# Weaving softmax steps into a 7-product matmul: later attention blocks, debits for mask sums, spread loads, and diagonal copies on GpSimd

## The chip, the core and the metric

The kernel runs on one core of one Trainium2 chip. A core has a matmul engine (TensorE, PE in the profile), two elementwise engines that do most of the rest (VectorE, DVE, and ScalarE, ACT), a third (GpSimd, POOL) and a sequencer that here only issues DMAs (SyncE, SP). Each engine works through its own instructions in order; across engines they wait for each other by semaphores. The metric is device time of one execution in microseconds.

## The reference

Windowed attention over 8 batches, 8 heads, 576 positions of 64 features, then a two-layer perceptron with an ELU on the 4608 resulting tokens of 512 features. All in float32.

```python
scores = scale * q @ k.T                                # per batch and head, 576 x 576
mask_plain = (rel >= 0) & (rel < 32)                    # heads 0 to 3, rel = row - column
mask_dil = (rel >= 0) & (rel < 32 * 4) & (rel % 4 == 0) # heads 4 to 7
scores = where(mask, scores, -1e9)
scores = scores - max(scores)
attn = exp(scores)
attn = attn / (sum(attn) + 1e-9)
x = (attn @ v), heads side by side: (4608, 512)
h = x @ w_in                                            # (512, 2048)
g = where(h > 0, h, exp(min(h, 0)) - 1)
out = g @ w_out                                         # (2048, 512)
```

## The kernel before, in words

Every float32 matmul is made of three matmuls of a shorter format (each operand is split into a rounded part, by a "cast", and a "rest"). The tokens come in two ways: three plain chunks of 512 tokens first, then four groups of 768 tokens (`superchunk(c)`, c = 0 to 3), of which this change concerns the first three.

In a group the first layer is done with seven products instead of eight, in Strassen's manner. There are 8 quarters q, each with 7 products s. `ORDER` names the weight combination of each (`A11 S2 S3 A12 S1 A22 S4`, DMA'd ahead into a ring of `r` tiles by `load_combined`, from the tensor `combined`), `MOVING` the token operand (`B11 T2 T3 B21 T1 T4 B22`). A product is six matmuls of 128x384; the products accumulate in PSUM in `x_ps` (tile `h`) or `y_ps` (tile `a_ps` or `h`). `TODO[s]` lists what follows product s on the other engines: `u1`, `u2`, `u3` are ScalarE copies out of PSUM, `C11`, `C22`, `C12` VectorE adds out of PSUM, `C21` a ScalarE copy; then exp, relu, cast on ScalarE and elu, rest on VectorE; `keep` sends half of the result to `aside` in memory. TensorE can start the next product into a PSUM tile when these reads are done. Products of the second layer (three matmuls of 128x512 each) wait in a list and are put between the others by `pop`. Behind the 8 quarters comes a loop of 16 steps f, in which the kept halves come back from `aside` (`bring`), are cast and rested (tiles `gh`, `gl`), and the operands of the next group are made (`OPERANDS[f]`).

The attention of batches 4 to 7 is woven into this. It is cut in 8 blocks, each of two head pairs; block i has a scores piece `S<i>` and an outputs piece `O<i>`. `PIECES[c]` says behind which product (index 7q+s) of group c a piece stands, `LATER` behind which f. An S piece puts the score matmuls (`o_ps<-kt,qt`, `a_ps<-kt,qt`) on TensorE; half way a GpSimd memset clears the first column of one `kt`, and the remaining score matmuls read it. Six VectorE adds of masks (L381) follow. The rest of the softmax is put in a list, `side`, by `later_probabilities`: per pair a maximum, a subtract, an exp on ScalarE, a sum, +1e-9, a reciprocal, a multiply, two 32x32-block transposes, and six copies of the diagonal blocks into a tile `pt`. The first pair uses tile `sm` and `pt_79`, the second tile `a` and `pt_78`. An O piece multiplies `pt` by `vt` (`a_ps<-pt,vt`).

What sets the order: `work(vec, act)`, once behind each product (`SPARE[s]` holds the two numbers, in us), adds `vec` to a running credit and runs steps from `side` as long as credit remains, and ScalarE steps within `act`. `work_all`, ahead of each piece, runs everything left of the blocks before it (of its own block too, for an O piece): a flush. `Ordered` (L430) ties each instruction it issues into this written order on its engine; that is why so many instructions of the profile have L430 as their line, and the matmuls L110.

q, k and v of later blocks are fetched by `load_qk` and `load_v`, at the end of an S or O piece: four or two DMAs at once on SyncE's queue, which carries the ring's and `aside`'s transfers, too.

Of the kernel before, what the change touches and what calls it, by code (L numbers as in the profile page):

```python
# [44 lines left out]
CS = 3  # L45
# [6 lines left out]
POPS = (2, 2, 0, 0, 0, 2, 0)  # L52
FIRST_POPS = (2, 2, 0, 0, 0, 0, 0)
TODO = [t.split() for t in ("u1 exp0< relu0< w0", "u2 elu0< cast1< cast0< rest1< rest0< w1", "u3 keep1< w2", "C11 w3", "C22 keep0< expR1 w4", "C21 expL1 relu1 w5 push1", "C12 elu1 w6 push0")]
SPARE = ((1.4, 0.45), (0.3, 0.9), (1.2, 1.3), (1.6, 1.7), (0.9, 0.5), (0.9, 0.0), (0.0, 0.45))
SOON = "cast:B11 make:T1 rest:B11 make:T2 cast:T2 rest:T2 make:T3 cast:T3 rest:T3".split()
FIRST = [t.split() for t in ("cast:B21 rest:B21", "make:T4 cast:T1 rest:T1", "cast:T4 rest:T4", "cast:B22 rest:B22", "", "", "")]
OPERANDS = [t.split() for t in ("", "", "", "cast:B11", "make:T1 rest:B11", "make:T2 cast:T2", "rest:T2 make:T3", "cast:T3 rest:T3", "cast:B21 rest:B21", "make:T4 cast:T1",
                                "rest:T1", "cast:T4 rest:T4", "cast:B22", "rest:B22", "", "")]
WHEN = {1: (0, 6, 7, 13), 2: (0, 6, 7, 12)}  # L60
EARLY = 14
LAST = 14
OPER = 12
PLAIN = ("a5", "a-1'")
BLOCKS = [(b, hp) for b in range(CS + 1, B) for hp in (0, 2)]
PIECES = {0: {14: "S1", 20: "O0", 28: "S2", 34: "O1", 42: "S3", 48: "O2"}, 1: {7: "S4", 28: "S5", 34: "O4", 48: "O5"}, 2: {7: "S6", 28: "S7", 34: "O6", 48: "O7"}}
LATER = {0: {3: "O3"}}
COMBINE = {(1, 11): 0, (1, 13): 1, (1, 15): 2, (2, 1): 3, (2, 4): 4, (2, 6): 5, (2, 9): 6, (2, 11): 7}

TINY = float(np.array([0x38000000], np.uint32).view(np.float32)[0])  # L70
# [3 lines left out]
def body(ctx: ExitStack, tc: tile.TileContext, q, k, v, masks, w_in, w_out, out):  # L74
# [184 lines left out]

    qk_of, v_of = {}, {}  # L260

    def load_qk(i):
        if i < B * NPAIR:
            qt, kt = qk_of[i] = ap.tile([P, S], F32, name="qt"), ap.tile([P, WINDOW + S], F32, name="kt")
            nc.sync.dma_start(out=qt, in_=q[i])
            nc.sync.dma_start(out=kt, in_=k[i])

    def load_v(i):
        if i < B * NPAIR:
            vt = v_of[i] = ap.tile([P, 2 * NU, D], F32, name="vt")  # L270
            nc.sync.dma_start(out=vt, in_=v[i])

    def score(to, qt, kt, h, n, c, start=True, stop=True):

# [154 lines left out]
        def __getattr__(self, name):  # L429
            return lambda *args, **kw: inorder(getattr(self.eng, name)(*args, **kw))  # L430

    vec, act = Ordered(nc.vector), Ordered(nc.scalar)
    side, credit, turn, latest = [], [0.0], [0], {}

    def run(n):
# [6 lines left out]
    def next_step(vec_free, act_free):  # L442

        seen = set()
        for n, (block, pair, copies, on_act, cost, step) in enumerate(side):
            when, where = latest.get((block, pair), (0, on_act))
            ready = (block, pair) not in seen and (where == on_act or when + where < turn[0]) and not (copies and block - 1 in made)
            seen.add((block, pair))
            if ready and (act_free if on_act else vec_free) > 0:
                return n  # L450
        return None

# [21 lines left out]
    def later_probabilities(b, hps, groups):  # L474

        other_sm = flat("a5", TOKENS, TOKENS + 2 * NU * 2 * G)[:QB, :].rearrange("p (u j) -> p u j", u=2 * NU)
        sms = [ap.tile([QB, 2 * NU, 2 * G], F32, name="sm", bufs=1), other_sm]
        for j in (1, 0):
            masks_added(hps[j], groups[j], sms[j], vec)
        small = [[ap.tile([QB, 2 * NU], F32, name=n, bufs=4) for n in ("nmx", "sums")] for _ in hps]  # L480
        trs = [transposed() for _ in hps]
        wide = lambda x: x.unsqueeze(2).broadcast_to([QB, 2 * NU, 2 * G])

        def steps(j):

            sm, (mx, sums), tr = sms[j], small[j], trs[j]
            yield False, False, 0.9, lambda: vec.tensor_reduce(out=mx, in_=sm, op=ALU.max, axis=mybir.AxisListType.X)
            yield False, False, 0.9, lambda: vec.tensor_tensor(out=sm, in0=sm, in1=wide(mx), op=ALU.subtract)
            yield False, True, 0.85, lambda: act.activation(out=sm, in_=sm, func=AF.Exp, scale=0.125)
            yield False, False, 0.9, lambda: vec.tensor_reduce(out=sums, in_=sm, op=ALU.add, axis=mybir.AxisListType.X)  # L490
            yield False, False, 0.15, lambda: vec.tensor_scalar(out=sums, in0=sums, scalar1=1e-9, scalar2=None, op0=ALU.add)
            yield False, False, 0.2, lambda: vec.reciprocal(out=sums, in_=sums)
            yield False, False, 0.9, lambda: vec.tensor_tensor(out=sm, in0=sm, in1=wide(sums), op=ALU.mult)
            for r in range(2):
                part = sm[:, :, r * G:(r + 1) * G]
                yield False, False, 0.57, lambda part=part: vec.transpose(out=part, in_=part)
            for r in range(2):
                for c in range(GU):
                    ks, cs, rs = slice((c + r) * G, (c + r + 1) * G), slice(c * G, (c + 1) * G), slice(r * G, (r + 1) * G)
                    yield True, True, 0.51, lambda ks=ks, cs=cs, rs=rs: act.copy(out=tr[ks, :, cs], in_=sm[cs, :, rs])  # L500

        block = BLOCKS.index((b, hps[0]))
        side.extend((block, j, *step) for j in range(2) for step in steps(j))
        return [(b, hp, tr) for hp, tr in zip(hps, trs)]

    def scores_piece(b, hps, between=lambda: None):

        s = three()

        def place(j, h, n0, n1):  # L510

            bank, o = (s[2], n0 + h * 4) if j and n0 < 4 else (s[h], n0 + 2 * j)
            return bank[:, o * 2 * G:(o + n1 - n0) * 2 * G]

        qk = [qk_of.pop(b * NPAIR + hp) for hp in hps]

        one, other = [(0, n) for n in range(NU)], [(1, n) for n in range(NU)]
        for i, (first_head, second_head) in enumerate(zip(other[1:4] + other[:1] + other[4:] + one, other[4:] + one + other[:4])):
            if i == 4:
                nc.gpsimd.memset(qk[1][1][:, :1], 0.0)  # L520
                between()
            for c in range(GU)[::-1 if i == 3 else 1]:
                for h, (j, n) in enumerate((first_head, second_head)):
                    score(place(j, h, n, n + 1), *qk[j], h, n, c)
        groups = [[[(n0, n1, place(j, h, n0, n1)) for n0, n1 in (((0, NU),), ((0, 4), (4, NU)))[j]] for h in range(2)] for j in range(2)]
        if b <= CS:
            made = [probabilities(*exponentials(b, hp, groups[j])) for j, hp in enumerate(hps)]
        else:
            made = later_probabilities(b, hps, groups)
        for hp in hps:  # L530
            load_qk(b * NPAIR + hp + 2)
        return made

    def outputs_piece(made):

        s = three()
        places = ((s[0], 0, 5), (s[1], 5, 6)), ((s[1][:, QB:], 0, 4), (s[2], 4, 6))
        for place, (b, hp, tr) in zip(places, made):
            products(place, v_of.pop(b * NPAIR + hp), tr)
        for place, (b, hp, _) in zip(places, made):  # L540
            if hp == 0:
                x32[b] = xp.tile([P, NPAIR, S], F32, name="x32", bufs=2)
            if b <= CS:
                copies(b, hp, place)
        if made[0][0] > CS:
            for j, i in ((1, 1), (0, 0), (0, 1), (1, 0)):
                copies(*made[j][:2], places[j][i:i + 1], inorder)
        for b, hp, _ in made:
            load_v(b * NPAIR + hp + 2)

    xh, xl = [None] * NC, [None] * NC
    xall = xp.tile([P, 2 * NC, TC], F32R, name="xall")
# [230 lines left out]
    def piece(what):  # L783
# [2 lines left out]
        b, hp = BLOCKS[i]  # L786
        work_all(i - (what[0] == "S"))
        if what[0] == "S":
            made[i] = scores_piece(b, (hp, hp + 1), lambda: pop(2))
        else:  # L790
            outputs_piece(made.pop(i))
# [6 lines left out]
    def superchunk(c):  # L798
        x_ps = y_ps = None
        for q in range(NQ):  # L800
            base = (c * NQ + q) * 7
            for s in range(7):
                load_combined(base + s + RING)
                if (c, s) == (0, 0) and q in (1, 2):
                    more_sets(q == 2)
                if s == 0:
# [37 lines left out]
        for f in range(NF):  # L844
            if f in LATER.get(c, ()):
                piece(LATER[c][f])
            bring(f + 2)
            gh, gl = g = next_set()
            w = arrivals[f % len(arrivals)]
            act.copy(out=gh, in_=w)  # L850
# [2 lines left out]
            if c + 1 < NSC:  # L853
                for what in OPERANDS[f]:
                    moving_operand(c + 1, what, vec, act)
            work(2.0, 0.9)
            pop(3 if f > 5 else 2)
        assert len(fifo) == 12, len(fifo)

# [81 lines left out]
    for c in range(CS):  # L941
# [14 lines left out]
        for f in range(NF):  # L956
# [46 lines left out]
                    next(first_late)  # L1003
            if (c, f) == (CS - 1, EARLY):
                made[0] = scores_piece(CS + 1, (0, 1), lambda: flush(LAG))
            flush(LAG - 1 - (f == NF - 1) if c == 0 and f >= NF - 2 else LAG if c < CS - 1 or f < NF - 1 else LAG + 1)
            if (c, f) in COMBINE:
                with tc.issue_after(low[-1]), tc.issue_after(high[-1]):
# [78 lines left out]
```

## Time and profile before

| what | value |
|---|---|
| time, median of 3 runs | 911.58 us (909.11 to 913.34) |
| the profiled execution's own time | 912.36 us |
| its span, first to last instruction | 910.6 us |
| mean granted TensorE clock | 0.989 |
| TensorE busy | 871.8 us, 96% |
| VectorE busy | 584.0 us, 64% |
| ScalarE busy | 529.4 us, 58% |
| GpSimd busy | 7.2 us, 24 instructions |

The first group's products run from about 340 us to 455 us, its loop over f to about 515 us; the second group starts there, the third near 657 us. A row of the timeline has the start, the length, the engine, the line, the operation and its tiles, and in brackets the idle time before it with what ended it. A row of groups has count, busy time and mean nanoseconds. The stretches list busy time and count of PE, weight loads, DVE, ACT and POOL, then the granted clock, the DMA share and GB/s.

### The profile page before, as it was taken

To read this page: it belongs to the slowest core of one execution; us is meant where nothing else is said; L and a number is where in the kernel's file an instruction comes from. 1 tells how busy PE (TensorE), PEld (TensorE's weight loads), DVE (VectorE), ACT (ScalarE), POOL (GpSimd) and SP (SyncE) were. 2 spreads that over 40 slices of the span, in tenths; PEclk is the share of its full clock that TensorE was granted. 3 is DMA by queue.
4 is the path that set the end of the run, shared out by engine and by line. 5 is a ranking of instruction groups with operands and counts; after the bars stand their busy time and mean duration, and the time that the engine had idled before them with its cause. 6 is when DMAs were issued, how large, how long until landed. Compare 5 with 4: busy or idle time off the path is not lost.

```text
span 910.6 us, 17336 instructions
## 1 busy us (share of the span) xinstructions
PE 871.8 (96%) x6752; PEld 719.5 (79%) x6752; DVE 584.0 (64%) x951; ACT 529.4 (58%) x1029; POOL 7.2 (1%) x24
## 2 busy tenths in 40 slices
PE   6999999999999998889999899999999999999998
PEld 4545677778868887778878798988888988999976
DVE  6999998777696967665854557445566537233331
ACT  3665675645645556668664575754485764455541
POOL 2000000000000000000000000000000000000000
PEclk8999999999999998999999999999999999999999
DMA  9996344224536256776753767652666653677541
GB/s 348 369 353 236 126 127 148 68 68 146 197 116 229 73 190 178 257 219 197 221 161 90 248 194 238 202 184 81 219 215 178 203 158 102 176 249 197 151 139 61
DMA packets 93457, 166.45 MB, mean 183 GB/s; under 512 B 9696, under 2 KB 40768, under 8 KB 93376
## 3 DMA queue, kind: packets, MB, share of 16 engines
q1 hardware_dynamic: 89200, 158.01, 55.1%
q10 hardware_dynamic: 4176, 7.34, 2.2%
q8 instruction: 53, 0.87, 0.4%
q14 instruction: 28, 0.23, 0.1%
HBM read 124.42 MB, written 40.89 MB: 182 GB/s over the span
## 4 chain that ended last, share of the span: by engine, by line
PE 70%; DVE 13%; ACT 9%; issue 4%; DMA 3%; SPq 1%; ACTq 0%; POOL 0%; DVEq 0%
PE o_ps L110 34%; PE h L110 29%; PE a_ps L110 6%; ACT a L430 2%; DVE a-1_3237 L430 2%; ACT pt L430 2%; DMA r<-combined 2%; DVE pt L417 1%; DVE sm L430 1%; ACT h L642 1%; DVE nmx L430 1%; DVE sm L312 1%; DVE nmx L394 1%; DVE r L430 1%; DVE sm L381 1%
## 5 line engine op out<-in xcount | busy, mean ns | idle before, releaser
L110 PE MATMUL h<-xall,r 128*128 128x384 f32 (+1 forms) x708 | 160.2, 367 | 16.7 <-DVE a-1_3237 L430 7.7
L110 PEld LDWEIGHTS h<-xall,r 128*128 128x128 f32 x708 | 128.2, 189 | 39.3 <-DVE a-1_3237 L430 12.0
L110 PE MATMUL o_ps<-a,gh 128*128 128x512 f32 x434 | 147.2, 433 | 0.7 <-ACT gh L611 0.7
L110 PE MATMUL h<-r,r 128*128 128x384 f32 x476 | 112.7, 347 | 2.4 <-ACT a-1_3237 L430 2.4
L110 PEld LDWEIGHTS o_ps<-a,gh 128*128 128x128 f32 x434 | 80.7, 188 | 31.3 <-issue 17.2
L430 DVE SCALAR_TENSOR_TENSOR a-1_3237<-a-1_3237,a 128x768 f32<-128x768 f32 x64 | 61.0, 954 | 54.8 <-ACT a L430 54.8
L430 ACT ACTIVATE a<-a-1_3237 128x384 f32<-128x384 f32 (+1 forms) x96 | 60.7, 632 | 58.4 <-DVE a-1_3237 L430 52.6
L110 PEld LDWEIGHTS h<-r,r 128*128 128x128 f32 x476 | 86.8, 193 | 6.5 <-ACT a-1_3237 L430 3.0
L430 ACT COPY e<-h 128x384 f32<-128x384 f32 x96 | 46.1, 480 | 76.2 <-PE h L110 75.4
L430 DVE TENSOR_TENSOR a-1_3237<-h,e 128x384 f32<-128x384 f32 x64 | 35.5, 554 | 71.6 <-PE h L110 71.6
L110 PE MATMUL o_ps<-r,gh 128*128 128x512 f32 x242 | 76.5, 397 | 0.7 <-ACT e L642 0.6
L110 PE MATMUL o_ps<-a,r 128*128 128x512 f32 x288 | 72.8, 394 | 0.0
L110 PE MATMUL o_ps<-a,gl 128*128 128x512 f32 x173 | 67.8, 392 | 0.7 <-DVE gl L612 0.7
L430 ACT ACTIVATE a<-a 128x768 f32<-128x768 f32 (+1 forms) x72 | 60.8, 844 | 3.8 <-DVE a L430 1.8
L110 PEld LDWEIGHTS o_ps<-a,r 128*128 128x128 f32 x288 | 54.2, 190 | 10.1
L110 PE MATMUL h<-a,r 128*128 128x384 f32 x256 | 60.5, 337 | 0.5 <-ACT e L430 0.5
L110 PEld LDWEIGHTS o_ps<-r,gh 128*128 128x128 f32 x242 | 45.2, 190 | 10.6 <-ACT e L642 1.1
L110 PEld LDWEIGHTS h<-a,r 128*128 128x128 f32 x256 | 46.1, 188 | 5.6 <-ACT e L430 1.8
L110 PE MATMUL o_ps<-r,gl 128*128 128x512 f32 x117 | 46.0, 393 | 0.3 <-DVE gl L430 0.3
L430 DVE TENSOR_TENSOR a-1_3237<-a_ps,e 128x384 f32<-128x384 f32 x32 | 17.7, 554 | 43.9 <-PE a_ps L110 43.9
L417 DVE STREAM_TRANSPOSE pt<-sm 32x384 f32<-32x384 f32 x72 | 40.9, 568 | 0.9
L110 PE MATMUL o_ps<-a,xall 128*128 128x512 f32 x153 | 40.0, 396 | 0.0
(197 smaller groups left out, 1470.2 us busy)
## 6 DMA issues: line engine op xcount, KB each, us to landing
r<-combined SPq DMA_DIRECT2D x224, 256.0 KB, 3.1
aside<-a-1_3237 SPq DMA_DIRECT2D x64, 192.0 KB, 3.2
vt<-v SPq DMA_DIRECT2D x30, 384.0 KB, 4.2
kt<-k SPq DMA_DIRECT2D x30, 304.0 KB, 4.6
qt<-q SPq DMA_DIRECT2D x30, 288.0 KB, 4.4
r<-w_in SPq DMA_DIRECT2D x16, 512.0 KB, 7.0
r<-w_out SPq DMA_DIRECT2D x16, 512.0 KB, 7.8
combined<-a SPq DMA_DIRECT2D x20, 256.0 KB, 3.1
```

Source lines behind the costliest of these rows:

```text
L110: return inorder(nc.tensor.matmul(*args, **kw))
L312: return keep(eng.tensor_tensor(out=sm, in0=sm, in1=sums.unsqueeze(2).broadcast_to([QB, 2 * NU, 2 * G]), op=ALU.mult))
L381: last = eng.tensor_tensor(out=sm[:, h * NU + n0:h * NU + n1, :].rearrange("p n j -> p (n j)"), in0=s_ps[:QB, :(n1 - n0) * 2 * G], in1=mas ...
L394: nc.vector.tensor_reduce(out=nmx, in_=sm, op=ALU.max, axis=mybir.AxisListType.X)
L417: last_transpose[b] = nc.vector.transpose(out=tr[ks, :, cs], in_=sm[cs, :, rs]).ins
L430: return lambda *args, **kw: inorder(getattr(self.eng, name)(*args, **kw))
L642: (nc.vector.tensor_copy if i else nc.scalar.copy)(out=o[:, s], in_=o_ps[:, s])
```

## The change

It does five things. (1) `SPARE` gives other allowances, an S piece takes 2.6 us off the credit and the first block's S piece, in the last plain chunk, 6.0 us; the loop over f gives 1.4/1.2 for f < 6 and 0.5/0.5 behind, instead of 2.0/0.9; `next_step` runs steps that cost nothing also at a credit of zero. (2) The pieces of the first group stand one quarter later, and O3 at f=6 instead of f=3; the operands for the next group start at f=5 instead of f=3. (3) The loads of later blocks are put in a list, and one is issued with every second product and every f. (4) The transposes and copies of a pair are done with r=1 first, and the three r=1 copies of each pair go to GpSimd. (5) The memset of `kt` goes through `Ordered`, too, so that it keeps its place among GpSimd's copies.

```diff
-SPARE = ((1.4, 0.45), (0.3, 0.9), (1.2, 1.3), (1.6, 1.7), (0.9, 0.5), (0.9, 0.0), (0.0, 0.45))
+SPARE = ((1.3, 0.0), (0.3, 0.9), (1.2, 1.0), (0.9, 1.7), (1.1, 0.0), (1.1, 0.0), (0.0, 0.45))
-OPERANDS = [t.split() for t in ("", "", "", "cast:B11", "make:T1 rest:B11", "make:T2 cast:T2", "rest:T2 make:T3", "cast:T3 rest:T3", "cast:B21 rest:B21", "make:T4 cast:T1",
-                                "rest:T1", "cast:T4 rest:T4", "cast:B22", "rest:B22", "", "")]
+OPERANDS = [t.split() for t in ("", "", "", "", "", "cast:B11 make:T1", "rest:B11", "make:T2 cast:T2", "rest:T2 make:T3", "cast:T3 rest:T3", "cast:B21 rest:B21",
+                                "make:T4 cast:T1", "rest:T1", "cast:T4 rest:T4", "cast:B22", "rest:B22")]
-PIECES = {0: {14: "S1", 20: "O0", 28: "S2", 34: "O1", 42: "S3", 48: "O2"}, 1: {7: "S4", 28: "S5", 34: "O4", 48: "O5"}, 2: {7: "S6", 28: "S7", 34: "O6", 48: "O7"}}
-LATER = {0: {3: "O3"}}
+PIECES = {0: {21: "S1", 27: "O0", 35: "S2", 41: "O1", 49: "S3", 55: "O2"}, 1: {7: "S4", 28: "S5", 34: "O4", 48: "O5"}, 2: {7: "S6", 28: "S7", 34: "O6", 48: "O7"}}
+LATER = {0: {6: "O3"}}
...
+    loads = []
+
+    def load_qk(i, later=False):
         if i < B * NPAIR:
             qt, kt = qk_of[i] = ap.tile([P, S], F32, name="qt"), ap.tile([P, WINDOW + S], F32, name="kt")
-            nc.sync.dma_start(out=qt, in_=q[i])
-            nc.sync.dma_start(out=kt, in_=k[i])
+            loads.append(lambda: nc.sync.dma_start(out=qt, in_=q[i]))
+            loads.append(lambda: nc.sync.dma_start(out=kt, in_=k[i]))
+        if not later:
+            load_next(2)
...
+    def load_next(n=1):
+
+        for _ in range(min(n, len(loads))):
+            loads.pop(0)()
...
-    vec, act = Ordered(nc.vector), Ordered(nc.scalar)
+    vec, act, pool = Ordered(nc.vector), Ordered(nc.scalar), Ordered(nc.gpsimd)
...
-            if ready and (act_free if on_act else vec_free) > 0:
+            if ready and (act_free if on_act else vec_free) > -1e-9 + (cost > 0) * 1e-6:
...
-            for r in range(2):
+            for r in (1, 0):
                 part = sm[:, :, r * G:(r + 1) * G]
                 yield False, False, 0.57, lambda part=part: vec.transpose(out=part, in_=part)
-            for r in range(2):
+            for r in (1, 0):
                 for c in range(GU):
                     ks, cs, rs = slice((c + r) * G, (c + r + 1) * G), slice(c * G, (c + 1) * G), slice(r * G, (r + 1) * G)
-                    yield True, True, 0.51, lambda ks=ks, cs=cs, rs=rs: act.copy(out=tr[ks, :, cs], in_=sm[cs, :, rs])
+                    if r:
+                        yield True, True, 0.0, lambda ks=ks, cs=cs, rs=rs: pool.tensor_copy(out=tr[ks, :, cs], in_=sm[cs, :, rs])
+                    else:
+                        yield True, True, 0.51, lambda ks=ks, cs=cs, rs=rs: act.copy(out=tr[ks, :, cs], in_=sm[cs, :, rs])
...
-                nc.gpsimd.memset(qk[1][1][:, :1], 0.0)
+                pool.memset(qk[1][1][:, :1], 0.0)
...
         if what[0] == "S":
+            credit[0] -= 2.6
             made[i] = scores_piece(b, (hp, hp + 1), lambda: pop(2))
...
                 load_combined(base + s + RING)
+                if s % 2 == 0:
+                    load_next()
...
             bring(f + 2)
+            load_next()
...
-            work(2.0, 0.9)
+            work(*((1.4, 1.2) if f < 6 else (0.5, 0.5)))
...
                 made[0] = scores_piece(CS + 1, (0, 1), lambda: flush(LAG))
+                credit[0] -= 6.0
```

How it moves instructions is seen at three places. On GpSimd, before, the memsets of `kt` for all S pieces followed one another:

```order
L312 TENSOR_TENSOR r_80<-r_80,sums 96x768 x2
L118 COPY r_281<-nmx 96x2
L520 MEMSET kt 128x1 x12
```

On GpSimd now; the first memset behind copies is that of S2, the second that of S3:

```order
L118 COPY r_281<-nmx 96x2
L441 MEMSET kt 128x1 x5
L441 COPY pt_79<-sm 32x12x32 x3
L441 COPY pt_78<-a_2131 32x12x32 x3
L441 MEMSET kt 128x1
L441 COPY pt_79<-sm 32x12x32 x3
L441 COPY pt_78<-a_2131 32x12x32 x3
L441 MEMSET kt 128x1
```

From S2 on the memset stands behind six copies of the block before.

VectorE before, ahead of the masks of S3 (`o_ps_4385` holds its scores, `h_4326` is the tile that C22 and C12 read, `a_2131` the second pair's softmax):

```order
L430 TENSOR_REDUCE sums<-a_2131 96x12
L430 TENSOR_TENSOR a-1_3237<-a_ps_4310,e 128x384
L430 TENSOR_SCALAR sums<-sums 96x12
L430 RECIPROCAL sums<-sums 96x12
L430 TENSOR_TENSOR a_2131<-a_2131,sums 96x768
L430 TENSOR_TENSOR a-1_3237<-h_4326,e 128x384
L430 STREAM_TRANSPOSE a_2131<-a_2131 96x12x32 x2
L430 TENSOR_TENSOR a-1_3237<-h_4326,e 128x384
L430 SCALAR_TENSOR_TENSOR a-1_3237<-a-1_3237,a_2131 128x768
L430 TENSOR_TENSOR a_2131<-o_ps_4385,masks_sb 96x256 x2
```

VectorE now, ahead of the masks of S3 (`o_ps_4478`, and `h_4409` for C22 and C12):

```order
L441 TENSOR_TENSOR a-1_3237<-h_4409,e 128x384
L441 TENSOR_TENSOR a_2131<-a_2131,nmx 96x768
L441 TENSOR_TENSOR a-1_3237<-h_4409,e 128x384
L441 SCALAR_TENSOR_TENSOR a-1_3237<-a-1_3237,a_2131 128x768
L441 TENSOR_REDUCE sums<-a_2131 96x12
L441 TENSOR_SCALAR sums<-sums 96x12
L441 RECIPROCAL sums<-sums 96x12
L441 TENSOR_TENSOR a_2131<-a_2131,sums 96x768
L441 STREAM_TRANSPOSE a_2131<-a_2131 96x12x32 x2
L441 TENSOR_TENSOR a_2131<-o_ps_4478,masks_sb 96x256 x2
```

The second pair's sum, reciprocal and multiply have moved from ahead of C22 and C12 to behind them, into the flush.

VectorE before, ahead of O5 in the second group (`h_5786` is read by C22 and C12):

```order
L430 TENSOR_TENSOR a_2131<-a_2131,sums 96x768
L430 TENSOR_TENSOR a-1_3237<-h_5786,e 128x384
L430 STREAM_TRANSPOSE a_2131<-a_2131 96x12x32 x2
L430 TENSOR_TENSOR a-1_3237<-h_5786,e 128x384
L430 SCALAR_TENSOR_TENSOR a-1_3237<-a-1_3237,a_2131 128x768 x2
```

VectorE now, ahead of O5 (`h_5877`):

```order
L441 TENSOR_TENSOR a_2131<-a_2131,sums 96x768
L441 STREAM_TRANSPOSE a_2131<-a_2131 96x12x32
L441 TENSOR_TENSOR a-1_3237<-h_5877,e 128x384
L441 SCALAR_TENSOR_TENSOR a-1_3237<-a-1_3237,a_2131 128x768
L441 STREAM_TRANSPOSE a_2131<-a_2131 96x12x32
```

The second transpose, which the three ScalarE copies of that pair need, has moved behind C12 and an elu.

More of the change, by code (lines that the diff above doesn't have):

```diff
@@ L260, in body, with load_v @@
     qk_of, v_of = {}, {}
-    def load_qk(i):
+    loads = []
+    def load_qk(i, later=False):
         if i < B * NPAIR:
             qt, kt = qk_of[i] = ap.tile([P, S], F32, name="qt"), ap.tile([P, WINDOW + S], F32, name="kt")
-            nc.sync.dma_start(out=qt, in_=q[i])
-            nc.sync.dma_start(out=kt, in_=k[i])
-    def load_v(i):
+            loads.append(lambda: nc.sync.dma_start(out=qt, in_=q[i]))
+            loads.append(lambda: nc.sync.dma_start(out=kt, in_=k[i]))
+        if not later:
+            load_next(2)
+    def load_v(i, later=False):
         if i < B * NPAIR:
             vt = v_of[i] = ap.tile([P, 2 * NU, D], F32, name="vt")
-            nc.sync.dma_start(out=vt, in_=v[i])
+            loads.append(lambda: nc.sync.dma_start(out=vt, in_=v[i]))
+        if not later:
+            load_next(2)
+    def load_next(n=1):
+        for _ in range(min(n, len(loads))):
+            loads.pop(0)()
     def score(to, qt, kt, h, n, c, start=True, stop=True):
@@ L530, in scores_piece @@
         for hp in hps:
-            load_qk(b * NPAIR + hp + 2)
+            load_qk(b * NPAIR + hp + 2, b > CS)
         return made
@@ L548, in outputs_piece @@
         for b, hp, _ in made:
-            load_v(b * NPAIR + hp + 2)
+            load_v(b * NPAIR + hp + 2, b > CS)
     xh, xl = [None] * NC, [None] * NC
```

## The prediction

> **What bounds the kernel now.** I read the page first, then busy time by stretches of 20 us, then what TensorE waited for from 340 us on (where the edited code begins to act), then the timelines round each wait.
>
> ```profile
> span 910.6 us, 17336 instructions
> PE 871.8 (96%) x6752; PEld 719.5 (79%) x6752; DVE 584.0 (64%) x951; ACT 529.4 (58%) x1029; POOL 7.2 (1%) x24
> 330.00:350.00 20.00, 17.05 (x151) 14.51 (x136) 15.80 (x27) 10.95 (x19) 0.00 (x0) 0.93 0.50 141
> 350.00:370.00 20.00, 20.00 (x228) 17.70 (x227) 9.44 (x16) 16.03 (x31) 0.10 (x1) 0.90 0.76 232
> 370.00:390.00 20.00, 17.67 (x127) 15.35 (x126) 16.38 (x28) 11.93 (x24) 0.00 (x0) 1.00 0.75 236
> 510.00:530.00 20.00, 16.32 (x77) 14.65 (x76) 14.13 (x23) 11.11 (x21) 0.00 (x0) 0.91 0.76 253
> 650.00:670.00 20.00, 17.03 (x81) 15.23 (x80) 15.07 (x24) 11.70 (x22) 0.00 (x0) 0.91 0.78 255
> PE h L110 <- DVE a-1_3237 L430: 7.7, 5, 2.1
> PE a_ps L110 <- ACT pt L430: 0.5, 1, 0.5
> ```
>
> TensorE (PE) is busy 96% of the span, so the change can win only what TensorE loses by waiting or by a lowered clock, and it loses whatever it newly makes TensorE wait for. In the rows by stretches the third number from the end is the granted clock. The time lost to it is 20 us times what is missing to 1: 1.4+2.0=3.4 us between 330 and 370, 1.8 at 510, 1.8 at 650. From 370 to 390 it was whole, as in all stretches up to 730 but those two. The waits that the change touches:
>
> ```profile
> 345.16 1.15 PE L110 MATMUL h<-xall,r 128*128 128x384 f32 x5 [1.40 <-DVE xall L430]
> 347.87 1.62 PE L110 MATMUL h<-xall,r 128*128 128x384 f32 x4 [1.56 <-issue]
> 379.01 1.31 PE L110 MATMUL h<-xall,r 128*128 128x384 f32 x6 [2.13 <-DVE a-1_3237 L430]
> 518.65 1.29 PE L110 MATMUL h<-xall,r 128*128 128x384 f32 x6 [2.48 <-DMA r<-combined]
> 521.13 2.29 PE L110 MATMUL h<-r,r 128*128 128x384 f32 x6 [1.20 <-ACT a-1_3237 L430]
> 658.94 1.28 PE L110 MATMUL h<-xall,r 128*128 128x384 f32 x6 [1.77 <-DMA r<-combined]
> 661.42 1.97 PE L110 MATMUL h<-r,r 128*128 128x384 f32 x5 [1.20 <-ACT a-1_3237 L430]
> 377.54 0.95 DVE L430 TENSOR_TENSOR a<-a,nmx 96x768 f32<-96x768 f32 x1
> 378.41 0.55 DVE L430 TENSOR_TENSOR a-1_3237<-h,e 128x384 f32<-128x384 f32 x1
> ```
>
> TensorE waits at 379.01 for the C22 add of 378.41, which stood behind a softmax subtract on VectorE (DVE); five such waits make the 7.7 us.
>
> **What it gains.** Lower vector allowances and the debits after an S piece put C22 ahead of the reductions behind every S piece: all five waits go, 7.7 us. If the reductions only land on another add, as little as half of it; I take all, since the order has them behind C22 in each place.
>
> First quarter of the first group: the waits at 345.16 and 347.87 (1.40+1.56) and their 3.4 us of low clock fall with the debit of 6.0, which takes five softmax steps away from ahead of the operands' rests; the casts on ScalarE (ACT) ahead of the first rest stay, so I leave 1.1 us. Gain 6.4-1.1=5.3 (bounds 3.0, one wait staying with half of the lowered clock, and 6.4).
>
> At S4 and S6 the ring load `r<-combined` now stands behind three attention loads instead of four, so I leave three quarters of 2.48+1.77, 3.2 us. The ScalarE wait (1.20 twice) came from the C21 copy standing behind output DMAs on ScalarE's queue; they now stand behind relu1, so it goes, and with it the lowered clock (3.6). Gain 6.65+3.6-3.2=7.0 (bounds 2, clock and loads unchanged, and 10.2, all of it). On SyncE the other q, k and v loads are spread and moved past ring loads, too; they are read whole products later, which costs nothing unless one lands over ten microseconds late. Gains: 7.7+5.3+7.0=20.0.
>
> **What it costs: S2 and S3.** Half of the diagonal copies go to GpSimd (POOL), and so does the `kt` memset, in program order. Ahead of S2 and of S3 the flush now has still to do the whole second half of pair 1's softmax, three GpSimd copies of it stand ahead of the memset, and TensorE's matmul that reads that `kt` waits for GpSimd. Before, the memset stood alone on its queue. The walk, from the start of the product before the piece (T=0 is 443.62; TensorE's own arrival is from S1, 363.33 to 367.22):
>
> ```profile
> 363.33 1.21 PE L110 MATMUL h<-r,r 128*128 128x384 f32 x6
> 367.22 0.22 PE L110 MATMUL o_ps<-kt,qt 64*32 64x64 f32 x1
> 443.62 1.33 PE L110 MATMUL h<-r,r 128*128 128x384 f32 x6
> 444.98 0.48 ACT L430 COPY e<-h 128x384 f32<-128x384 f32 x1
> 445.36 0.85 ACT L430 ACTIVATE a<-a-1_3237 128x768 f32<-128x768 f32 x1
> 446.24 0.85 ACT L430 ACTIVATE a<-a 128x768 f32<-128x768 f32 x1
> L430 ACT COPY pt<-a 32x384 f32<-32x384 f32 x48 | 24.4, 508 | 0.6
> L430 ACT ACTIVATE a<-a 96x768 f32<-96x768 f32 x8 | 6.6, 830 | 1.8 <-DVE a L430 1.8
> L430 DVE TENSOR_REDUCE sums<-a 96x12 f32<-96x768 f32 x8 | 7.2, 906 | 0.0
> L430 DVE TENSOR_SCALAR sums<-sums 96x12 f32<-96x12 f32 x16 | 2.6, 160 | 0.0
> L430 DVE RECIPROCAL sums<-sums 96x12 f32<-96x12 f32 x16 | 3.6, 224 | 0.6
> L430 DVE TENSOR_TENSOR a<-a,sums 96x768 f32<-96x768 f32 x8 | 7.6, 954 | 0.3
> L430 DVE STREAM_TRANSPOSE a<-a 96x384 f32<-96x384 f32 x16 | 8.3, 550 | 0.0
> L312 POOL TENSOR_TENSOR r<-r,sums 96x768 f32<-96x768 f32 x2 | 2.9, 1470 | 2.6 <-ACT pt L367 2.2 <-DVE sums L311 0.4
> L97 POOL MEMSET pt<- 128x1152 f32 x2 | 2.1, 1059 | 0.3 <-POOLq L1078 0.3
> L118 POOL COPY r<-nmx 96x2 f32<-96x2 f32 x3 | 0.6, 185 | 11.7 <-DVE nmx L340 11.7
> L520 POOL MEMSET kt<- 128x1 f32 x12 | 1.2, 99 | 665.4 <-PE o_ps L110 360.3 <-PE h L110 305.1
> ```
>
> ScalarE: u1 to 1.84, exp0 to 2.59, relu0 to 3.47, two copies to `pt_79` (2 x 0.51) to 4.49, the softmax exp (0.83) to 5.32. VectorE: sum 0.91, +1e-9 0.16, reciprocal 0.22, multiply 0.95, first transpose 0.55: 8.1. Then three GpSimd copies of 384 elements. No row has one: the 96x2 copy gives at least 0.19 each, the two-operand 96x768 row whole 1.47 at most. By the memset rows (99 ns fixed, 0.83 ns an element) it would be 0.42, by the two-operand row at half size 0.78; a copy reads one operand, where these read none and two, so I take the middle, 0.60. The Trainium skill ("GPSIMD Engine Reference", section 3.1) has 769 ns for 512 elements, an estimate of 0.58 here, with which the wait would be 0.06 shorter; no run yet shows it. The memset ends at 8.1+1.8+0.1=10.0. TensorE reaches its matmul at 367.22-363.33=3.9: it waits 6.1 us (bounds 4.9 and 8.7), and nothing but this queue is behind it, since TensorE works in order. A wait of 2.48+1.20 brought one lowered stretch of 1.8; this one is longer, so I add 1.8. Cost of S2 and S3: 2 x 7.9 = 15.8.
>
> **O3, O5, O7.** O3 moves from f=3 to f=6, but its block's steps move more.
>
> ```profile
> 455.20 2.01 PE L110 MATMUL o_ps<-r,r 128*128 128x512 f32 x8
> 464.39 1.21 PE L110 MATMUL a_ps<-pt,vt 128*64 128x96 f32 x24
> 465.06 0.56 DVE L430 TENSOR_TENSOR gl<-r,gh 128x384 fp32r<-128x384 f32 x1 [2.03 <-DMA a-1_3237<-aside]
> 585.75 0.56 DVE L430 TENSOR_TENSOR a-1_3237<-h,e 128x384 f32<-128x384 f32 x1 [2.86 <-PE h L110]
> 586.22 0.95 DVE L430 SCALAR_TENSOR_TENSOR a-1_3237<-a-1_3237,a 128x768 f32<-128x768 f32 x1
> ```
>
> TensorE comes to O3 after 18 more matmuls at 0.23 (455.20: eight in 2.01, overlapped), at 464.39+4.1=468.5, and does the 24 products with `pt_79` until 469.7. The steps, from the second arrival's `gl` on VectorE (ends 465.6): two transposes to 466.7, three `pt_79` copies 1.5, a cast 0.5 (the size of a copy), the exp 0.83, a cast 0.5 on ScalarE: 470.1; a rest and two makes of 0.55, then sum to multiply 2.2, two transposes 1.1: 475.0; three ScalarE copies: 476.6. Wait 6.9 (4.4 if the casts run beside it, 7.6 with a late arrival), 1.8 of clock, less the 0.54 waited there before: 8.2.
>
> O5 and O7: the order puts C12 and an elu (rows 585.75, 586.22) between the two transposes, and three ScalarE copies last. From the product's end: 0.56+0.95+0.55+1.5=3.6, against 1.2 of `pt_79` products: 2.4 wait each (2.0 to 3.0). The waits of 2.1 at 379 left the clock at 1.00, that of 2.48 with 1.20 did not; I count three quarters of 1.8. 2 x (2.4+1.35)=7.5.
>
> The 48 copies moved off ScalarE (508 ns each) save it 24 us; it is 58% busy, so that counts only inside the flush, above. The next group's operands start at f=5 instead of f=3, and the last rest, of B22, stands at f=15; the first product needs B11, which is ready nine steps earlier, and the product with B22 is the seventh, so I cost the shift at nothing; if that cover is gone, a rest of 0.55 and a cast of 0.5 stand once ahead of TensorE in each of two groups, 2 us.
>
> **Sum.** Costs 15.8+8.2+7.5=31.5, gains 20.0: +11.5. The profiled execution took 912.4, which gives 923.9; the median of the runs shown is 0.8 lower, so 923. About 0.5% (907.0 to 916.1) is what a measurement of this kernel can tell from no change.
>
> **The rivals.**
>
> The cover holds: the flush ends before TensorE arrives, because VectorE has free time in the quarter ahead (9.44 busy of 20 at 350) and its steps run sooner than the order's neighbours suggest. Only the gains are left: 911.6-20.0=892. It decides the sign where the flush ends 3.8 us sooner at all three places, S2, S3 and O3 (3 x 3.8=11.5). Against it: the exp stands behind relu0 of a product that TensorE has just begun, on the same in-order queue. Chance 0.12, between 887 (all upper bounds of the gains) and 906.
>
> The waits come, the lowered clock doesn't: 5 lowered stretches fewer, 3 x 1.8+2.7=8.1: 915, at the edge of no change. Against it: the wait that kept 1.00 was 2.13, and these are three times as long. Chance 0.12, half of it within 0.5%.
>
> GpSimd is dear: 1.47 a copy lengthens S2 and S3 by 2.6 each: 928, and behind it O5 and O7 with more clock 930 to 936. For it: POOL rows are few here. Chance 0.13.
>
> A rule against my count at O5 and O7: the clock falls only after a whole idle window, so waits of 2.4 us cost none: 923-2.7=920, in the forecast's own range, chance 0.3 within it. That is how the Trainium skill ("TensorE: Matmul & The Clock Gate", "What's actually happening") tells it: half rate after at least one idle window of about 3.4 us. The trace differs: at 518 to 521 two idles of 2.48 and 1.20, with 1.29 of matmuls between them, were enough for 0.91.
>
> **Chances.** My forecast's case 0.58 (its own range 917 to 930), the dear GpSimd 0.13, no lowered clock 0.12, cover 0.12, the gains cut and the costs cut together 0.05 (within 0.5%). Slower: 0.58+0.13+0.06=0.77. Same: 0.06+0.05=0.11. Faster 0.12. The range leaves out the cover and the far end of the dear case: 911 to 933.
>
> **What would show it.** PE rows `o_ps<-kt,qt` with about 6 us of idle, released by POOL, near 412 and 444 (80.3 us for the 35 products from 363.33 to 443.62), and a granted clock near 0.9 there; `a_ps<-pt,vt` with about 7 us released by ACT `pt` near 470 and 2.4 us twice later; no C22 wait of 2.1; shorter DMA waits at S4 and S6, without the ScalarE one; POOL copies near 0.6 us. The prediction is wrong if the kt matmul's wait is under 3 us, or if GpSimd's copies finish before TensorE comes.

## The result and the profile after

The changed kernel takes 923.08 us (median of 4 runs, 921.30 to 923.74), the kernel before beside it 911.88: ratio 1.0123, 95% interval 1.0094 to 1.0152. The forecast was 923, slower. The profiled execution took 923.74; its page begins:

```profile
span 922.0 us, 17363 instructions
PE 874.3 (95%) x6752; PEld 724.9 (79%) x6752; DVE 587.3 (64%) x951; ACT 504.5 (55%) x981; POOL 39.1 (4%) x72
```

ScalarE has 25 us less to do and GpSimd 32 us more, yet the span is 11.4 us longer. What TensorE waited for from 340 us on:

```profile
PE o_ps L110 <- POOL kt L441: 12.2, 2, 6.1
PE a_ps L110 <- POOL pt L441: 6.3, 1, 6.3
PE a_ps L110 <- ACT pt L441: 5.2, 2, 2.6
PE h L110 <- DMA r<-combined: 4.1, 4, 1.5
PE h L110 <- issue: 0.7, 1, 0.7
```

Of the old list only the ring loads are left, 4.1 us against 4.3: no C22 wait, no ScalarE C21 wait, and at 344 us 0.7 where 1.40 and 1.56 stood. Three new entries, 23.7 us together, take its place. The same waits in TensorE's timeline (S2, O3, O5; S3 and O7 look like S2 and O5):

```profile
344.79 1.28 PE L110 MATMUL h<-xall,r 128*128 128x384 f32 x6 [0.69 <-issue]
406.71 0.31 PE L110 MATMUL o_ps<-kt,qt 64*32 64x64 f32 x1 [6.11 <-POOL kt L441]
476.66 1.55 PE L110 MATMUL a_ps<-pt,vt 128*64 128x96 f32 x16 [6.34 <-POOL pt L441]
594.05 1.23 PE L110 MATMUL a_ps<-pt,vt 128*64 128x96 f32 x12 [2.60 <-ACT pt L441]
```

Busy time by stretches; the third number from the end is again the granted clock:

```profile
330.00:350.00 20.00, 19.27 (x110) 16.66 (x96) 12.89 (x23) 11.48 (x20) 0.00 (x0) 1.00 0.59 171
390.00:410.00 20.00, 13.89 (x200) 12.40 (x199) 11.61 (x24) 8.65 (x16) 3.73 (x7) 0.83 0.44 125
430.00:450.00 20.00, 13.89 (x193) 12.02 (x192) 9.34 (x19) 9.36 (x17) 2.29 (x5) 0.83 0.48 145
470.00:490.00 20.00, 13.66 (x76) 11.27 (x73) 11.74 (x21) 8.42 (x17) 1.50 (x3) 0.83 0.33 99
590.00:610.00 20.00, 17.40 (x118) 15.69 (x117) 6.84 (x11) 9.14 (x19) 2.13 (x3) 0.91 0.58 160
670.00:690.00 20.00, 20.00 (x99) 18.56 (x99) 14.70 (x25) 13.19 (x24) 4.30 (x6) 0.94 0.73 216
730.00:750.00 20.00, 17.40 (x118) 15.66 (x117) 7.90 (x14) 10.73 (x22) 2.14 (x3) 0.91 0.44 136
```

Each stretch with a new wait has TensorE idle and a lowered clock. The walk to S2 can be followed on ScalarE, VectorE and GpSimd:

```profile
399.85 1.03 ACT L441 COPY pt<-sm 32x384 f32<-32x384 f32 x2
400.90 0.84 ACT L441 ACTIVATE a<-a 96x768 f32<-96x768 f32 x1
401.78 0.95 DVE L441 TENSOR_REDUCE sums<-a 96x12 f32<-96x768 f32 x1 [3.70 <-ACT a L441]
403.22 0.95 DVE L441 TENSOR_TENSOR a<-a,sums 96x768 f32<-96x768 f32 x1
404.21 1.03 DVE L441 STREAM_TRANSPOSE a<-a 96x384 f32<-96x384 f32 x2
404.92 1.58 POOL L441 COPY pt<-a 32x384 f32<-32x384 f32 x3 [9.35 <-DVE a L441]
406.56 0.10 POOL L441 MEMSET kt<- 128x1 f32 x1
```

VectorE stood idle 3.70 us for the exp, which stood behind two copies and a relu on ScalarE; from there it is one chain to the memset, and TensorE starts 0.05 us after it.

### The profile page after: what moved, and what is told of

It reads as the page before. It is cut to its first block, busy times and chain, and to the rows that moved or that the text cites. A ratio compares the mean times of both kernels' runs of the same rounds, so it can differ in the third digit from the quotient of the medians.

```text
span 922.0 us, 17363 instructions
## 1 busy us (share of the span) xinstructions
PE 874.3 (95%) x6752; PEld 724.9 (79%) x6752; DVE 587.3 (64%) x951; ACT 504.5 (55%) x981; POOL 39.1 (4%) x72
## 5 line engine op out<-in xcount | busy, mean ns | idle before, releaser
L110 PE MATMUL h<-xall,r 128*128 128x384 f32 (+1 forms) x708 | 158.2, 364 | 5.4 <-DMA r<-combined 2.9
L110 PEld LDWEIGHTS o_ps<-a,r 128*128 128x128 f32 x288 | 54.0, 190 | 10.2
L110 PE MATMUL a_ps<-pt,vt 128*64 128x96 f32 x576 | 29.3, 256 | 11.7 <-POOL pt L441 6.3
```

Of the source, the lines that this page charges most:

```text
L110: return inorder(nc.tensor.matmul(*args, **kw))
```

## The experiments

Each was timed beside the kernel before on the same chip; ratios are against that.

**e1_hold: the flush's GpSimd copies behind the memset.**

```diff
+            if hold is not None and side[0][3] and side[0][4] == 0.0:
+                hold.append(side.pop(0)[5])
...
-            made[i] = scores_piece(b, (hp, hp + 1), lambda: pop(2))
+            made[i] = scores_piece(b, (hp, hp + 1), lambda: release(hold))
```

Ahead of an S piece `hold` keeps the GpSimd copies of the flush back; `release`, behind the memset, issues them and then does the `pop(2)`.

> The changed kernel, but ahead of an S piece the GpSimd copies of the flush are issued behind the memset of kt instead of ahead of it. Theory A (the starved softmax steps are the cause; whichever queue they end on, something of TensorE waits for them): the 6.1 us wait of the kt matmul goes at S2 and S3, but the masks now wait for the copies into pt_78 and the next product into a_ps for the masks: a new wait of 3.7 to 4.2 us, released by DVE, at both, and the clock still falls. 923 - 2 x 2.1 = 919 (916 to 921). Rival B (GpSimd, with the memset behind its copies, is the cause): both waits and their clock go, 2 x 7.7 = 15.4 us, 908.

918.20 us, ratio 1.0093 (1.0062 to 1.0123). The kt matmuls wait no more; but a little later in the same quarter TensorE stops for 3.69 us. TensorE, then ScalarE, at S2:

```profile
407.42 1.01 PE L110 MATMUL h<-a,r 128*128 128x384 f32 x2 [3.69 <-ACT e L441]
405.32 1.55 ACT L441 COPY pt<-a 32x384 f32<-32x384 f32 x3 [3.53 <-DVE a L441]
406.89 0.48 ACT L441 COPY e<-h 128x384 f32<-128x384 f32 x1
```

The size fits theory A, the place doesn't: not the masks hold TensorE, but `u2`, the ScalarE copy out of PSUM, which stands behind three `pt_78` copies that wait for the transposes. GpSimd's queue was only the first of two in-order queues that the flush had filled; taking it away uncovers the second, 2.4 us shorter.

**e2_spare: larger allowances, meant to leave the flush nothing to do.** GpSimd copies, ordered memset, places and loads are those of the change. VectorE's numbers in `SPARE` add up to 8.0 us a quarter instead of 5.9 (the expectation has 5.6 to 7.7); three of ScalarE's numbers and the debit are raised with them.

```diff
-SPARE = ((1.3, 0.0), (0.3, 0.9), (1.2, 1.0), (0.9, 1.7), (1.1, 0.0), (1.1, 0.0), (0.0, 0.45))
+SPARE = ((1.4, 0.5), (0.3, 0.9), (1.2, 1.0), (1.5, 1.7), (2.0, 0.5), (1.6, 0.5), (0.0, 0.45))
-            credit[0] -= 2.6
+            credit[0] -= 3.05
```

> The changed kernel with larger allowances (5.6 to 7.7 us of VectorE a quarter, the debit 3.05 instead of 2.6), so that nothing is left to flush at any piece; the GpSimd copies and their memset stay. Theory A: the waits at S2, S3 (6.1 each), O3 (6.3), O5 and O7 (2.6 each) go with their lowered clock, 23.8 and some 6 of clock: 893 (890 to 898). Rival B: GpSimd's copies still cost: 908 or more. Rival C (the gain of the debits and the cost of the flush are the same work in two places, so the C22 and C12 waits come back): 893+7.7, 901 or more.

894.67 us, ratio 0.9829 (0.9794 to 0.9863), 27 to 28 us under the changed kernel. TensorE's waits now:

```profile
PE h L110 <- DMA r<-combined: 2.9, 4, 0.9
PE a_ps L110 <- POOL pt L441: 2.8, 1, 2.8
PE h L110 <- ACT a-1_3237 L441: 1.2, 1, 1.2
```

The waits at S2, S3, O5 and O7 are gone, that at O3 is down from 6.3 to 2.8, so something is still flushed there, and one C22 wait of 0.7 and a ScalarE wait of 1.2 came back. At S2 and S3 the same GpSimd copies with the same memset behind them cost nothing as soon as the steps ahead are done in time: rivals B and C fall. Which of the raised numbers did it, VectorE's, ScalarE's or the debit, was not separated.

**e4_credit: the two debits alone, in the kernel before.**

```diff
+            credit[0] -= 2.6
...
+                credit[0] -= 6.0
```

The first stands at every later S piece, the second behind the first block's.

> The kernel before with the two debits alone (2.6 at an S piece, 6.0 behind the first block's), all copies on ScalarE, old places and old loads. Theory A: the five C22 waits and the waits at 344 to 348 go (13 us with clock), but 13 to 16 steps a block are left to flush at S1, S2 and S3 and some at O3, O5 and O7; the kt matmul doesn't wait, yet a_ps does for the masks, 4 to 6 us at S2 and S3, and O3, O5 and O7 wait for ScalarE copies 2 to 5 us: no gain in all, 911 to 923. Rival B: without GpSimd no cost is left, 899.

933.70 us, ratio 1.0255 (1.0221 to 1.0289), 22.9 us slower, 11 beyond the range expected.

```profile
PE h L110 <- ACT e L430: 15.8, 3, 6.3
PE a_ps L110 <- ACT pt L430: 14.6, 3, 6.6
```

Of the C22 waits at most 0.2 is left, and the one at 344 is 0.7, as expected. But with all six copies of a pair on ScalarE TensorE waits for the `u` copy of the new quarter, 3.4 at S1 and 6.3 and 6.1 at S2 and S3; O3 waits 6.6, O5 and O7 4.0 each. I had sized the S waits at 4 to 6 and taken the masks as their end. Without any GpSimd copy the debits alone cost twice what the whole change does.

**e5_pool: the GpSimd copies alone, in the kernel before** (the hunks on `pool`, `r in (1, 0)` and `next_step` of the diff).

> The kernel before with the GpSimd copies alone (r=1 first, three copies a pair on GpSimd, memset in order behind them). Theory A: the steps are done before the piece, the copies of 0.5 to 0.7 us lie beside other work, the kt matmul doesn't wait: no change within 0.5%, 909 to 913. Rival B: a new wait of several us at S2 and S3 (and at S5, S7), 918 or more.

902.37 us, ratio 0.9912 (0.9881 to 0.9943): neither theory had a gain of 8.5 us. The C22 waits; S1's masks and C22 on VectorE; two of the stretches that had 0.93 and 0.91 before. The first row is S1's masks in the kernel before:

```profile
370.25 0.75 DVE L430 TENSOR_TENSOR a<-o_ps,masks_sb 96x256 f32<-96x256 f32 x2 [3.92 <-ACT pt L430]
PE h L110 <- DVE a-1_3237 L430: 3.7, 5, 0.8
365.85 0.75 DVE L430 TENSOR_TENSOR a<-o_ps,masks_sb 96x256 f32<-96x256 f32 x2 [3.04 <-PE o_ps L110]
374.01 0.55 DVE L430 TENSOR_TENSOR a-1_3237<-h,e 128x384 f32<-128x384 f32 x1
330.00:350.00 20.00, 17.03 (x156) 14.48 (x141) 16.09 (x28) 10.97 (x19) 0.13 (x1) 1.00 0.46 141
650.00:670.00 20.00, 18.49 (x94) 16.62 (x95) 13.24 (x23) 14.92 (x27) 4.06 (x6) 1.00 0.75 245
```

The masks wait for TensorE's scores instead of ScalarE's copies, so everything behind them on VectorE, C22 too, comes sooner, and the five waits fall from 7.7 to 3.7 us. That is 4.0 of the 8.5; the wait of 0.54 at O3 is gone, too. Part of the rest is the clock, which was lowered at 347 and 661 us before and not here, though the waits there (1.40 and 1.56; 1.99 and 1.20) are no shorter; at 510 it is lower here, 0.83 against 0.91. That part need not be the copies' doing (see the last section). What is theirs can be seen in the quarter of S1, where neither clock is lowered: TensorE takes 19.06 us for it before (363.33 to 382.39) and 16.89 here (361.10 to 377.99); S2's and S3's quarters are 2.1 us shorter, too, 6.3 us in all.

**e6_actcopies: the changed kernel with the copies back on ScalarE** (the memset stays where the change has it).

```diff
-                    if r:
-                        yield True, True, 0.0, lambda ks=ks, cs=cs, rs=rs: pool.tensor_copy(out=tr[ks, :, cs], in_=sm[cs, :, rs])
-                    else:
-                        yield True, True, 0.51, lambda ks=ks, cs=cs, rs=rs: act.copy(out=tr[ks, :, cs], in_=sm[cs, :, rs])
+                    yield True, True, 0.51, lambda ks=ks, cs=cs, rs=rs: act.copy(out=tr[ks, :, cs], in_=sm[cs, :, rs])
```

> The changed kernel with all diagonal copies back on ScalarE (the memset has GpSimd to itself again). Theory A as it stands after the first four runs (the debits leave steps to the flush, and GpSimd copies shorten the flush): slower than the changed kernel, since ScalarE now does six copies a pair in the flush: about 6.2 of wait for the ScalarE copy out of PSUM at S2 and S3, 4 at O5 and O7 instead of 2.6, more at O3: 928 (924 to 935). Rival B (the GpSimd queue is the cause): faster than before, about 900.

931.83 us, ratio 1.0240 (1.0191 to 1.0288).

```profile
PE a_ps L110 <- ACT pt L441: 18.3, 4, 7.0
PE h L110 <- ACT e L441: 12.7, 2, 6.4
```

As expected of theory A, slower than the change: 931.8 against 923.1, or 21.4 against 11.2 over the kernel before beside each. With the debits GpSimd's copies are thus worth 8.8 to 10.2 us, about what they are worth without (8.5), and rival B is refuted from both sides. O5 and O7 wait 5.0 us each, not 4.

**e3_loads: the spread loads alone, in the kernel before** (the hunks on `loads` and `load_next`).

> The kernel before with the loads of later blocks put in a list and issued singly, nothing else. Theory A: the waits for ring loads at S4 and S6 fall from 2.48 and 1.77 to about 1.5 each, the two ScalarE waits of 1.20 stay or turn into waits for a load, and the clock falls as before at one or both: 909 (907 to 911.5). Rival D (the load burst is the cause of all of it): 2.48+1.77+2 x 1.20 and two lowered stretches of 1.7, 10 us, go: 901.

912.18 us, ratio 1.0015 (0.9987 to 1.0043): no change, just above my range; rival D falls as well.

```profile
PE h L110 <- DVE a-1_3237 L441: 10.3, 7, 2.1
PE h L110 <- ACT a-1_3237 L441: 3.6, 2, 1.9
```

The waits for `r<-combined` are gone altogether, yet TensorE stops at the same places: for C22 (1.3, two more of these waits than before) and for the C21 copy (1.6 and 1.9 instead of 1.2 each). The load had only been the last of three things to arrive.

**e8_best: e2_spare with the loads of the second and third group spread further.**

```diff
-                if s % 2 == 0:
+                if (s % 2 == 0) if c == 0 else (s in (2, 6) and (q, s) != (1, 2)):
```

> e2_spare with the loads of the second and third group spread further (two a quarter, at products 2 and 6, instead of one with every second product). Theory A: the four waits for ring loads left there (0.51, 0.82, 0.86, 0.71) go: 894.7-2.9=892 (890.5 to 893.5). Rival: they are set by the ring's own traffic: no change, 894.7.

894.60 us, ratio 0.9837 (0.9777 to 0.9897): the rival's value, though that the ring's own traffic is the reason is not shown. The four waits add up to 3.0 us against 2.9, one of them now for a VectorE step.

**e9_best: small allowances only while the first block's steps run, more in the loop over f, O3 a step later.**

```diff
+MORE = ((1.4, 0.5), (0.3, 0.9), (1.2, 1.0), (1.5, 1.7), (2.0, 0.5), (1.6, 0.5), (0.0, 0.45))
...
-                        work(*SPARE[s])
+                        work(*(SPARE if (c, q < 3) == (0, True) else MORE)[s])
...
-LATER = {0: {6: "O3"}}
+LATER = {0: {7: "O3"}}
...
-            work(*((1.4, 1.2) if f < 6 else (0.5, 0.5)))
+            work(*((2.0, 1.2) if f < 7 else (0.5, 0.5)))
```

`SPARE` is the change's, `MORE` is that of e2_spare. It keeps e8_best's loads and its debit of 3.05.

> e8_best with the changed kernel's own small allowances in the first three quarters of the first group, 2.0 instead of 1.4 of VectorE in the loop over f below 7, and O3 at f=7. Theory A: the waits of 0.74, 1.17 and 0.28 in the first group's second quarter and the 2.76 at O3 go, 4.9 us: 887 (885 to 890). Rival: the steps pushed together in the loop delay the next group's operands, and the start of the second group waits: 890 or more.

887.86 us (887.00 to 888.69), ratio 0.9757 (0.9711 to 0.9804): faster than both kernels.

```profile
span 886.9 us, 17365 instructions
PE h L111 <- DMA r<-combined: 3.3, 4, 1.3
PE h L111 <- issue: 0.7, 1, 0.7
```

Ring loads behind S4 and S6 are nearly all that TensorE still waits for in the three groups.

## Why the prediction was right, point by point

**S2 and S3** (6.1 of wait and 1.8 of clock each): 6.11 twice, released by GpSimd's memset of `kt`. The queue argument held because every row of the walk lay in the profile of before; only the GpSimd copies were a guess, 0.60 between bounds of 0.19 and 1.47. That it held to a tenth of a microsecond is partly luck: from the product's start (396.46) the copies begin at 8.5 us, not 8.1, three of them take 1.6, not 1.8, and TensorE arrives at 4.1, not 3.9. Both groups of copies after:

```profile
L441 POOL COPY pt<-a 32x384 f32<-32x384 f32 x24 | 16.5, 687 | 68.5 <-DVE a L441 67.9
L441 POOL COPY pt<-sm 32x384 f32<-32x384 f32 x24 | 15.4, 643 | 192.9 <-DVE sm L441 161.2 <-ACT a-1_3237 L441 31.0
```

0.64 to 0.69 on the mean; 0.53 ahead of S2 (three in 1.58, while ScalarE makes three copies of its own and VectorE is all but idle). The estimate from the Trainium skill's figure ("GPSIMD Engine Reference", section 3.1), 0.58, lies between.

**O3** (6.9 of wait): 6.34. The profile names GpSimd's copies as what ended it, but they end at 476.23 and ScalarE's last `pt_78` copy at 476.56, 0.1 us before TensorE starts, as the walk had it. **O5 and O7** (2.4 each): 2.60. I counted three quarters of a lowered stretch; both had one (0.91, that is 1.8). So the rival by the page "TensorE: Matmul & The Clock Gate" of the Trainium skill, which asks for a whole idle window of about 3.4 us, fails here: 2.60 was enough, twice (the last section says when it is).

**C22** (7.7 gained): no such wait is left, and more came of it. S1's quarter, 19.06 us before, takes 15.88 (368.99 to 384.87); 2.33 of the difference is idle time, the rest is TensorE's busy time for the same matmuls, 16.73 before and 15.88 now, which the prediction left out. The three S quarters make 9.5 us, the two C22 waits of the second and third group 0.9 each. **First quarter** (5.3 gained, 1.1 left): 0.69 left at a clock of 1.00.

**S4 and S6** (7.0 gained, 3.2 left): with C22 the term that was mis-sized. 6.65 us of waits became 4.1, all for ring loads, and the lowered stretch went at S4 but not at S6 (0.94 from 670 to 690): 2.6+1.8=4.4 gained, not 7.0. e3_loads shows that the deferral brings nothing by itself; what was gained here needed C21 and C22 out of the way as well. (The second and third group's first products start at 491.89 and 632.90 in the kernel before; 515 and 657 are where the waits at S4 and S6 lie.)

**The clock at S2, S3 and O3** (1.8 each) was taken as one lowered stretch. The rows have 0.83, 3.4 us, twice as much. But part of the lowered time lies inside the wait, where it costs nothing. At S2 it is more than half. Stretches round its wait of 400.60 to 406.71, inside it and behind it, and last the one behind S3's wait of 435.74 to 441.85:

```profile
400.00:402.50 2.50, 0.60 (x50) 0.44 (x41) 0.72 (x1) 1.71 (x3) 0.00 (x0) 1.00 0.48 166
403.00:406.50 3.50, 0.00 (x0) 0.00 (x0) 2.17 (x4) 1.20 (x3) 1.50 (x3) 0.50 0.01 2
406.75:409.50 2.75, 2.75 (x52) 2.58 (x53) 1.43 (x5) 0.08 (x1) 0.00 (x0) 0.50 0.24 41
410.00:412.50 2.50, 2.50 (x14) 2.27 (x13) 2.12 (x4) 1.57 (x4) 0.00 (x0) 1.00 0.95 304
441.85:447.30 5.45, 5.45 (x58) 4.80 (x59) 3.98 (x9) 1.59 (x4) 0.00 (x0) 0.50 0.52 157
```

By TensorE's timeline S1's quarter, which has no wait, goes from 368.99 to 384.87 and S2's from 396.46 to 420.01: 7.67 longer, of which 6.11 are the wait and 1.56 the clock, against 7.9 forecast. At S3 only 1.4 of the 6.8 lowered us lie inside the wait, and the same stretch of products is 8.79 longer (368.99 to 377.61 at S1, 431.59 to 449.00 at S3): 2.68 for the clock.

**The sum** came out at +11.4 on the span, forecast +11.5. Set against each other by the starts of the same 128x384 products of TensorE in both profiles, the terms are:

| term | forecast, us | by TensorE's timeline, us |
|---|---|---|
| first quarter | -5.3 | -5.4 |
| C22 | -7.7 | -11.3 |
| S4 and S6 | -7.0 | -4.1 |
| S2 and S3 | +15.8 | +16.5 |
| O3 | +8.2 | +7.5 |
| O5 and O7 | +7.5 | +8.7 |
| ahead of the first group | 0 | -0.6 |

C22 and S4 with S6 were missed by 3.6 and 2.9 us, one way each. (S2 and S3 are set against S1's quarter; O2's own 2.2 us are taken off the loop's time for O3; the column adds up to 11.3.) That the mechanism and its places were right is the prediction's; that the sum is right to a tenth is luck.

**What the prediction did not see:** it priced the copies moved off ScalarE at nothing outside the flush. e5_pool and e6_actcopies put them at 8.5 to 10.2 us of gain. Part of it was in the sum all the same: the walks were made with three ScalarE copies instead of six, and the C22 waits, which e5_pool halves without any debit, were all put down to the debits. And it took the order as it stood: that the loss was in the allowances and the debit, and that 27 to 28 us lay there, only e2_spare shows.

**Where the 11 us come from.** Alone, the debits cost 22.9, the GpSimd copies gain 8.5, the spread loads do nothing measurable. That leaves 14.4; the change as a whole has 11.2. The difference, the lowered allowances and the later pieces weren't separated; the parts overlap at the same waits.

## What to carry to other kernels

Work that is put off to free an engine must fit before its deadline: count what a debit takes out of each interval against what the interval has to do, and look at what is left for the flush. A flush costs what its longest in-order queue holds back, and taking one queue out uncovers the next, as 6.1 us became 3.7; doing the steps in time removes both. A small instruction that TensorE needs should not share a queue with copies that wait for something else, unless these are known to be early.

## What was not expected of the hardware

The clock is not lowered by the length of a wait alone. The kernel before waited 2.13 ahead of 379.01 and kept 1.00; e3_loads waited 2.14 for the same C22 add and had 0.91:

```profile
376.94 1.31 PE L110 MATMUL h<-xall,r 128*128 128x384 f32 x6 [2.14 <-DVE a-1_3237 L441]
370.00:390.00 20.00, 17.86 (x120) 16.17 (x121) 14.93 (x25) 11.13 (x22) 0.00 (x0) 0.91 0.69 214
```

In e5_pool the waits of 1.40 and 1.56 left the clock whole, which in the kernel before went with 0.93 and 0.90. This fits a window that runs freely against the program (the Trainium skill, "TensorE: Matmul & The Clock Gate", "What's actually happening", says so), with a threshold below a whole idle window. The traces show the phase, too. In the clock record of each profile the lowered stretches begin whole multiples of 3.41 us from one another; in the kernel before, those at 347.02, 521.11 and 661.05 are 51 and 41 of them apart. Cut along this grid, the two waits look like this, first the kernel before, then e3_loads:

```profile
374.32:377.73 3.41, 2.57 (x12) 1.95 (x12) 3.34 (x6) 0.85 (x1) 0.00 (x0) 1.00 0.93 308
377.73:381.15 3.42, 2.14 (x28) 1.89 (x30) 2.65 (x4) 2.12 (x4) 0.00 (x0) 1.00 0.29 95
374.92:378.34 3.42, 1.40 (x10) 1.16 (x12) 2.84 (x5) 1.49 (x4) 0.00 (x0) 1.00 0.53 171
378.34:381.75 3.41, 3.41 (x46) 3.41 (x46) 2.19 (x5) 1.56 (x3) 0.00 (x0) 0.50 0.41 96
```

Before, the wait is split between two windows, 0.84 and 1.28 us idle, and the clock stays whole; in e3_loads one window has 2.0 us of it, and the next is lowered. The changed kernel's two waits of 2.60 lay in one window each; e8_best's of 2.71 at O3 was split into 1.54 and 1.17 and kept 1.00. Over the ten profiles, from 320 to 800 us, each of the 30 full-clock windows with 1.85 us or more of TensorE idle was followed by a lowered one, none of the 1321 with less than 1.60, and 3 of the 5 between. So in this program about half a window of idle time is enough, and for a wait of 2 to 3 us its place on the grid matters as much as its length. A wait of about 2 us is thus a chance of 1.7 us more, and one of 6 us had a lowered clock every time.
